# First pair of heads loaded in whole rows and routed in two halves, with a shorter centroid norm and other places for the weight-rounding steps

## The chip, the cores and the metric

One core of a Trainium2 chip runs the whole kernel. The metric is the device time of one execution in microseconds (us), the median of several runs. The engines are named as the profile names them: PE (TensorE, with PEld for its weight loads), DVE (VectorE), ACT (ScalarE), POOL (GpSimd) and SP (the queue from which most DMAs are issued).

## The reference

Routing attention is followed by an MLP mixer. The attention has batch 4, 8 heads, 768 positions and head size 64. Each head has 16 centroids, and a query sees only the keys that have the same nearest centroid.

```python
c_n = centroids / (np.linalg.norm(centroids, axis=-1, keepdims=True) + 1e-06)
q_assign = np.argmax(np.einsum('bhsd,hcd->bhsc', q_n, c_n), axis=-1)
k_assign = np.argmax(np.einsum('bhsd,hcd->bhsc', k_n, c_n), axis=-1)
mask = q_assign[:, :, :, None] == k_assign[:, :, None, :]
scores = np.where(mask, scale * np.matmul(q, k.transpose(0, 1, 3, 2)), -1000000000.0)
attn = softmax(scores)          # written out in the reference
x = np.matmul(attn, v)          # then (B, S, H*D) = (4, 768, 512)
u = x + (np.maximum(x.transpose(0, 2, 1) @ w_tok1, 0.0) @ w_tok2).transpose(0, 2, 1)
out = u + np.maximum(u @ w_ch1, 0.0) @ w_ch2
```

Here q_n and k_n are q and k divided by their norms (which does not change the argmax), w_tok1 is 768x256, w_tok2 256x768, w_ch1 512x1536 and w_ch2 1536x512.

## The kernel before

The order of all instructions is written out by hand. Each engine works its own queue in that order.

**Pairs and groups.** Attention works on 16 pairs (a batch and two heads, both on the 128 partitions of a tile). A pair is done in four groups, numbered m over the whole kernel: g = m // 4 is the pair and s = m % 4 the step in it. Groups s = 0 and 1 handle the first half of the queries (qh = 0) with key chunks 0 to 2 and 3 to 5; s = 2 and 3 do the same for the second half. One group m issues, on PE, the score matmuls of three key chunks (scores, L377: a bf16 product of one-hot tiles "ohT" that sets the mask, then the fp32 product of q and k from "qkT"); on ACT, their exponentials (L383); on DVE, the sum of the exponentials of group m - 1 (add_up, L394 and L398); and on PE the product of those exponentials with v (values, L408). Scores live in a PSUM pool of three two-bank buffers, tag "sc", which are taken in turn; a fourth tile in some groups ("small" at s = 1, "px" at s = 2) shifts the turn by one, so that the third score block of the next group takes the buffer that this tile had.

**Routing of the next pair** runs beside the groups of the present one. At s = 0 turn transposes q and k in 32x32 blocks on DVE (L287). At s = 1 route_products multiplies them with the centroids (L299, into small). At s = 2 route takes the products through a DVE transpose (L316), a maximum (L320) and comparisons (L324) to one-hot rows, and counts the keys' entries on ACT (L331); then route_turn transposes the one-hots by a DMA on SP. The output of the previous pair is finished at the same steps: denominators into small (L425) at s = 1, their transpose (dent, L429) and reciprocal at s = 2, the transposes of the output (px, L438) at s = 2, and half_out (L446), which reads px on DVE, at the start of s = 3. load(g + 2) issues the loads of the pair after next at s = 1.

**Weights** are rounded beside attention. A step of weight_steps issues one raw load on SP for one piece, two ACT instructions (L200, L202) for the piece before it, and three DVE instructions (L207, L212, L217) and one POOL addition (L224) for the one before that. There are 19 pieces in the first list, hence 21 steps. A step is issued at the end of a group:

```python
if m < last - GROUPS:
    n = m % WEVERY == 0 or m == 1
else:
    n = m % 2 if m < last else 2
```

with WEVERY = 3, last = 64 and GROUPS = 4.

**The start.** begin loads the centroids and the first pair, computes the centroids' norm with an integer first guess and three Newton rounds (centroids_norm, L241 to L278), and routes the first pair ahead of group 0: turn for k, products, turn for q, route for k, products for q, and so on, with PE transposes of the one-hots (route_turn_first, L347) in place of the DMA. The first pair's loads are like all others: head size is split in two, so that a quarter of the partitions takes rows of 32 numbers (128 bytes). Matmuls on zeros (keep_warm, L729) stand between the steps.

After attention come the token products (tok1, L478; tok2, L487) and the channel products (L609, L660).

Of the kernel before, what the change touches and what calls it, by code (L numbers as in the profile page):

```python
# [17 lines left out]
C = 16  # L18
P = 128
# [15 lines left out]
GROUPS = 2 * NJ // NG  # L35
WEVERY = 3
SM_SCALE = 0.125
# [10 lines left out]
def kernel(  # L48
# [70 lines left out]
    rcps = const.tile([P, NPAIR, 2, 2, HJ], F32, name="rcps")  # L119
    cells = const.tile([P, NPAIR], F32, name="cells")  # L120

# [9 lines left out]

    def load(g, queues=None):


        b, f = divmod(g, NF)
        st = state.setdefault(g, {})
        st["qk"] = qkpool.tile([P, 2, NJ, NQ, QP], F32, name="qk")
        st["va"] = loads.tile([P, 2, NJ, D], F32, name="va")
        for a, src in ((1, k), (0, q)):
            queue = queues[a] if queues else nc.sync  # L140
            for c in range(NQ):
                h, d0 = 2 * f + c // 2, (c % 2) * QP
                queue.dma_start(
                    st["qk"][c * QP : (c + 1) * QP, a].rearrange("r j i d -> r (j i) d"),
                    src[b, h, :, d0 : d0 + QP].rearrange("(i r j) d -> r j i d", i=NQ, j=NJ),
                )
# [94 lines left out]
    def centroids_norm(cen):  # L241
        sq = rsmall.tile([P, D], F32, name="censq")
        ss = rsmall.tile([P, 1], F32, name="ss")
        nc.vector.tensor_tensor(out=sq, in0=cen, in1=cen, op=ALU.mult)
        nc.vector.reduce_sum(out=ss, in_=sq, axis=AX.X)

        lo = rsmall.tile([P, 1], F32, name="lo")
        nc.vector.tensor_scalar_max(out=lo, in0=ss, scalar1=float(2.0**-100))
        nrm = rsmall.tile([P, 1], F32, name="nrm0")
        nc.vector.tensor_scalar(  # L250
            out=nrm.bitcast(I32), in0=lo.bitcast(I32), scalar1=0.5, scalar2=float(0x1FBD1DF5),
            op0=ALU.mult, op1=ALU.add,
        )
        for it in range(3):
            rr = rsmall.tile([P, 1], F32, name="rr")
            nc.vector.reciprocal(out=rr, in_=nrm)
            tw = rsmall.tile([P, 1], F32, name="tw")
            nc.vector.scalar_tensor_tensor(
                out=tw, in0=ss, scalar=rr, in1=nrm, op0=ALU.mult, op1=ALU.add
            )  # L260
            nrm = rsmall.tile([P, 1], F32, name="nrm")
            nc.vector.tensor_scalar(
                out=nrm, in0=tw, scalar1=0.5, scalar2=(1e-6 if it == 2 else 0.0),
                op0=ALU.mult, op1=ALU.add,
            )
        rden = rsmall.tile([P, 1], F32, name="rden")
        nc.vector.reciprocal(out=rden, in_=nrm)
        cn = rsmall.tile([P, 2, D], F32, name="cn")
        for i in range(2):
            nc.vector.tensor_scalar_mul(out=cn[:, i], in0=cen, scalar1=rden)  # L270
        pc = ps_sc.tile([P, H * C], F32, tag="sc", name="pc")
        nc.tensor.transpose(out=pc, in_=cn.rearrange("p i d -> p (i d)"), identity=ident)
        nc.vector.tensor_copy(out=cnT, in_=pc)
        nc.vector.memset(cnd, 0.0)
        for i in range(2):
            rows = slice(i * D, (i + 1) * D)
            nc.vector.tensor_copy(
                out=cnd[rows, :, i], in_=cnT.rearrange("p (f i c) -> p f i c", f=NF, i=2)[rows, :, i]  # L278
            )


    def turn(g, kinds=(1, 0)):
        st = state[g]
        if 1 in kinds:
            st["T"] = qktp.tile([P, 2, NJ, P], F32, name="qkT")
        for a in kinds:
            nc.vector.transpose(  # L287
                out=st["T"][:, a].rearrange("p j t -> p (j t)"),
                in_=st["qk"][:, a].rearrange("p j i d -> p (j i d)"),
            )  # L290

    def route_products(g, a0=0, a1=2, pr=None):

        st, f = state[g], g % NF
        if pr is None:
            pr = ps_sc.tile([P, (a1 - a0) * NJ * QP], F32, tag="sc", name="pr")
        for i in range(NQ):
            rows = slice(i * QP, (i + 1) * QP)
            nc.tensor.matmul(  # L299
                pr[rows], lhsT=cnd[:, f].rearrange("p i c -> p (i c)"),  # L300
                rhs=st["T"][:, a0:a1, :, rows].rearrange("p a j r -> p (a j) r"),
                start=True, stop=True,
            )
        st["pr"] = pr

    def route(g, a0=0, a1=2):

        st = state[g]
        NR = (a1 - a0) * NJ * 2
        sc = rsmall.tile([P, NR, C], F32, name="sim")
        nc.vector.transpose(  # L316
            out=sc.rearrange("p n c -> p (n c)"), in_=st.pop("pr")
        )
        mx = rsmall.tile([P, NR], F32, name="mx")
        nc.vector.reduce_max(out=mx, in_=sc, axis=AX.X)  # L320
        for a in range(a0, a1):
            oh = ohs[g % 2][:, a].rearrange("p j (h x) -> p j h x", h=2)[:, :, :, 0:C]
            n = slice((a - a0) * 2 * NJ, (a - a0 + 1) * 2 * NJ)
            nc.vector.tensor_tensor(  # L324
                out=oh, in0=sc[:, n].rearrange("p (j h) c -> p j h c", h=2),
                in1=mx[:, n].rearrange("p (j h) -> p j h", h=2).unsqueeze(3)
                .to_broadcast([P, NJ, 2, C]),
                op=ALU.is_lt if a else ALU.is_ge,
            )
            if a:  # L330
                nc.scalar.activation(  # L331
                    out=rsmall.tile([P, NJ, 2, C], BF16, name="others"), in_=oh, func=ACT.Copy,
                    accum_out=cells[:, g : g + 1],
                )
            else:
                nc.vector.tensor_scalar_mul(out=oh, in0=oh, scalar1=-BIG)

# [8 lines left out]

    def route_turn_first(a):  # L347

        st, oh = state[0], ohs[0]
        if a == 1:  # L350
            st["ohT"] = qktp.tile([P, 2, NJ, P], BF16, name="ohT")
        po = ps_sc.tile([P, NJ, P], BF16, tag="sc", name="po")
        for j in range(NJ):
            nc.tensor.transpose(out=po[:, j], in_=oh[:, a, j], identity=identb)
        if a == 0:
            nc.vector.tensor_copy(out=st["ohT"][:, 0], in_=po)
        else:
            nc.scalar.copy(out=st["ohT"][:, 1], in_=po)

# [6 lines left out]
    def scores(m):  # L366
# [4 lines left out]

        for chunks in (range(NG - 1), (NG - 1,)):
            for src, start in ((st["ohT"], True), (st["T"], False)):
                for i in chunks:
# [307 lines left out]
    def fits():  # L682
# [4 lines left out]
        for i, (src, limit, op) in enumerate(  # L687
            (
                (flat, LIMIT, ALU.is_le),
                (flat, 1.0 / LIMIT, ALU.is_ge),  # L690
                (cells, float(2 * NJ * (C - 1)), ALU.is_equal),
            )
# [18 lines left out]
    def begin():  # L711
        cen = rsmall.tile([P, D], F32, name="cen")
        nc.sync.dma_start(cen, centroids.rearrange("h c d -> (h c) d"))
        load(0, (nc.scalar, nc.sync))

        nc.vector.memset(ones, 1.0)
        warm = rsmall.tile([P, WMAX], BF16, name="warm")
        nc.vector.memset(warm, 0.0)
        nc.scalar.activation(out=rsmall.tile([P, QP], F32, name="expd"), in_=ones, func=ACT.Exp)
        make_identity(nc, ident)  # L720
# [6 lines left out]
        def keep_warm(n):  # L727
            for _ in range(n):
                nc.tensor.matmul(pw, lhsT=warm[:, 0:P], rhs=warm[:, P : P + HS], start=True, stop=True)  # L729

        keep_warm(12)
        centroids_norm(cen)
        keep_warm(7)
        turn(0, (1,))
        route_products(0, 1, 2)
        turn(0, (0,))
        route(0, 1, 2)
        keep_warm(1)
        route_products(0, 0, 1)
        keep_warm(2)  # L740
        route_turn_first(1)
        route(0, 0, 1)
        keep_warm(1)
        route_turn_first(0)

# [9 lines left out]
    for m in range(last + 3):  # L755
# [3 lines left out]
        if s == 2:  # L759
            if old >= 0:  # L760
                pair_denominators(old)
            if more:
                route(g + 1)
            if old >= 0:
                pair_reciprocals(old)
        if s == 3 and old >= 0:
            for qh in range(2):
                half_out(old, qh)
        if more and s == 0:
            turn(g + 1)  # L770
        if 1 <= m <= last:
            add_up(m - 1)
        if m < last:
            scores(m)
        if 1 <= m <= last:
            values(m - 1)
        if m < last and s == 1:
# [3 lines left out]
            if more:  # L781
                route_products(g + 1, pr=two[:, 1, 0:HS])
        if more and s == 2:
# [24 lines left out]
        if m < last - GROUPS:  # L808
            n = m % WEVERY == 0 or m == 1
        else:  # L810
            n = m % 2 if m < last else 2
# [247 lines left out]
```

## Time and profile before

| | |
|---|---|
| Median of 3 runs | 896.99 us (895.4, 896.99, 897.04) |
| Profiled execution | span 895.3 us |
| PE busy | 873.7 us, 98% of the span |
| DVE, ACT, POOL busy | 499.4, 286.4 and 44.6 us |
| First score matmul | 15.49 us |
| Last of attention's value products | about 352 us |
| Mean granted PE clock | 0.993 of full speed |

A line of the profile gives, in order, the source line, the engine, the instruction, "output<-input" by tile names, the shapes, the count, the busy time and the mean of one, and then the engine's idle time ahead of it with what ended that. A timeline line gives the start and the length in us and then the same names. PE's busy time counts pipelined matmuls with modelled ends, so a high share says that PE is occupied, not that it runs at its peak. PEclk is the share of full clock that PE was granted.

### The profile page before, as it was taken

What the parts mean: (1) busy time and instruction counts of PE and PEld (TensorE: products, weight loads), DVE (VectorE), ACT (ScalarE), POOL (GpSimd) and SP (SyncE); (2) the same over time, 40 slices, a digit from 0 to 9 for tenths busy, and PEclk for the clock granted to TensorE, in tenths of its full rate; (3) what the DMA queues carried; (4) which work ended last, traced back from release to release, by engine and by line L of the source; (5) the groups of instructions that cost most, each with busy time, mean ns of one, the idle gap of its engine ahead of it and who ended that gap; (6) DMA issues with size and microseconds to landing.
All of it is one profiled execution on the core that took longest, in us unless ns stands there. A gap on an engine that the chain in (4) does not pass through costs nothing.

```text
span 895.3 us, 11001 instructions
## 1 busy us (share of the span) xinstructions
PE 873.7 (98%) x4286; PEld 519.4 (58%) x4286; DVE 499.4 (56%) x849; ACT 286.4 (32%) x501; POOL 44.6 (5%) x40
## 2 busy tenths in 40 slices
PE   7999999999999999999999999999999999999996
PEld 3444444444444444444458677686776867768675
DVE  5677778788788776385473434433344333443342
ACT  2554555555556545231120221202212022130210
POOL 1010000010101001140000000000000000000000
PEclk7999999999999999999999999999999999999999
DMA  9654455555665131130000001000010000100001
GB/s 164 138 107 89 89 120 113 112 123 106 106 120 100 40 89 34 61 118 0 1 0 1 1 24 47 1 1 0 17 54 0 1 1 13 59 1 1 0 25 50
DMA packets 136347, 47.61 MB, mean 53 GB/s; under 512 B 125152, under 2 KB 129248, under 8 KB 136288
## 3 DMA queue, kind: packets, MB, share of 16 engines
q1 hardware_dynamic: 133152, 46.45, 23.7%
q10 hardware_dynamic: 3136, 0.39, 0.4%
q8 instruction: 35, 0.57, 0.3%
q14 instruction: 24, 0.20, 0.1%
HBM read 34.64 MB, written 6.29 MB: 46 GB/s over the span
## 4 chain that ended last, share of the span: by engine, by line
PE 93%; DVE 5%; DMA 1%; ACT 0%; issue 0%; DVEq 0%
PE sc L377 16%; PE pX L660 14%; PE pX L609 14%; PE av L408 14%; PE pZ L660 7%; PE pZ L609 7%; PE ph L478 5%; PE pu L487 5%; PE pY L660 3%; PE pY L609 3%; DVE sum L398 2%; PE small L425 1%; PE pt L550 1%; PE small L299 1%; PE px L438 1%; DMA qk<-in_k_dram 1%
## 5 line engine op out<-in xcount | busy, mean ns | idle before, releaser
L383 ACT ACTIVATE ex<-sc 128x768 f32<-128x768 f32 x192 | 144.2, 809 | 59.8 <-PE sc L377 50.3
L377 PE MATMUL sc<-qkT 64*128 64x384 f32 x768 | 146.1, 486 | 0.0
L408 PE MATMUL av<-ex,va 128*64 128x384 f32 x768 | 137.8, 494 | 0.0
L398 DVE TENSOR_TENSOR sum<-sum,ex 128x768 f32<-128x768 f32 x128 | 124.4, 972 | 10.6 <-DVE sum L398 0.5
L408 PEld LDWEIGHTS av<-ex,va 128*64 128x64 f32 x768 | 49.5, 136 | 80.5 <-issue 66.0
L377 PEld LDWEIGHTS sc<-qkT 64*128 64x128 f32 x768 | 70.6, 189 | 34.6 <-issue 13.8
L609 PE MATMUL pX<-uT,wc 128*128 128x384 f32 x192 | 67.4, 487 | 0.0
L377 PE MATMUL sc<-ohT 64*128 64x384 bf16 x384 | 53.4, 329 | 6.0 <-DVE x L446 5.3
L617 ACT COPY p<-pX 128x384 f32<-128x384 f32 x24 | 11.4, 475 | 148.1 <-PE pX L609 148.1
L609 PEld LDWEIGHTS pX<-uT,wc 128*128 128x128 f32 x192 | 36.2, 190 | 24.7 <-issue 1.0
L224 POOL TENSOR_TENSOR wc<-wT,wup 128x512 int32<-128x512 int32 x24 | 32.5, 1354 | 244.4 <-DVE wT L217 194.7
L377 PEld LDWEIGHTS <-ohT 64*128 64x128 bf16 x384 | 13.8, 94 | 49.0 <-issue 32.2
L487 PE MATMUL pu<-h,wt 128*128 128x512 f32 x96 | 42.0, 592 | 0.0
L478 PE MATMUL ph<-x,wt 128*128 128x512 f32 x96 | 42.0, 593 | 0.0
L429 DVE STREAM_TRANSPOSE dent<-small 128x384 f32<-128x384 f32 x15 | 8.7, 583 | 55.9 <-PE small L299 50.5
L504 DVE TENSOR_TENSOR c<-pZ,u 128x384 f32<-128x384 f32 x24 | 13.4, 558 | 47.2 <-PE pZ L609 47.2
L504 DVE TENSOR_TENSOR x<-pX,x 128x256 f32<-128x256 f32 x24 | 10.2, 424 | 49.3 <-PE pX L660 49.3
L504 DVE TENSOR_TENSOR hA<-pY,p 128x384 f32<-128x384 f32 x24 | 13.4, 557 | 40.4 <-PE pY L609 40.4
L660 PE MATMUL pX<-w2s,hA 128*128 128x256 f32 x144 | 35.1, 380 | 0.5 <-DVE x L504 0.5
L660 PE MATMUL pX<-wc,hA 128*128 128x256 f32 x144 | 35.0, 379 | 0.0
L660 PE MATMUL pZ<-w2s,hS 128*128 128x256 f32 x144 | 35.0, 379 | 0.0
L660 PE MATMUL pY<-wc,hA 128*128 128x256 f32 x144 | 35.0, 379 | 0.0
(123 smaller groups left out, 1201.6 us busy)
## 6 DMA issues: line engine op xcount, KB each, us to landing
raw<-in_moe_w_ch_dram SPq DMA_DIRECT2D x24, 512.0 KB, 4.3
qk<-in_k_dram SPq DMA_DIRECT2D x64, 96.0 KB, 4.5
va<-in_v_dram SPq DMA_DIRECT2D x16, 384.0 KB, 3.2
out_dram<-x SPq DMA_DIRECT2D x24, 256.0 KB, 2.0
qk<-in_q_dram SPq DMA_DIRECT2D x60, 96.0 KB, 3.7
raw<-in_moe_w_tok_dram SPq DMA_DIRECT2D x3, 512.0 KB, 5.2
raw<-in_moe_w_tok_dram SPq DMA_DIRECT2D x4, 384.0 KB, 4.1
qk<-in_q_dram ACTq DMA_DIRECT2D x4, 96.0 KB, 4.4
```

Source lines behind the costliest of these rows:

```text
L224: nc.gpsimd.tensor_tensor(out=dst.bitcast(I32), in0=T, in1=up, op=ALU.add)
L299: nc.tensor.matmul(pr[rows], lhsT=cnd[:, f].rearrange("p i c -> p (i c)"), rhs=st["T"][:, a0:a1, :, rows].rearrange("p a j r -> p (a j) r" ...
L377: nc.tensor.matmul(scs[i][:, h, 0:HS], lhsT=src[rows, 1, j0 + i], rhs=src[rows, 0, js], start=start, stop=not start,)
L383: nc.scalar.activation(out=ex, in_=scs[i][:, :, 0:HS], func=ACT.Exp, scale=SM_SCALE)
L398: nc.vector.tensor_tensor(out=acc, in0=acc, in1=ex, op=ALU.add)
L408: nc.tensor.matmul(st["av"][h * D : (h + 1) * D], lhsT=st["va"][:, h, j], rhs=ex[:, h], start=(j == 0), stop=(j == NJ - 1),)
L478: nc.tensor.matmul(pf, lhsT=W["tok1"][:, j, t * P : (t + 1) * P], rhs=xs[b][:, j], start=(j == 0), stop=(j == NJ - 1),)
L487: nc.tensor.matmul(pu, lhsT=W["tok2"][:, t, j], rhs=h1s[b][:, t], start=(t == 0), stop=(t == NT - 1))
L504: nc.vector.tensor_tensor(out=dst, in0=a, in1=b, op=ALU.add)
L609: nc.tensor.matmul(psum, lhsT=A[a][:, k, c * P : (c + 1) * P], rhs=R[r][:, k], start=start and k == 0, stop=k == 1, skip_group_check=not s ...
L617: nc.scalar.copy(out=kept[name], in_=psum)
L660: nc.tensor.matmul(psum, lhsT=h2[a][:, k, i * P : (i + 1) * P], rhs=Bw[w][:, 3 * part + k], start=start and k == 0, stop=k == 2, skip_grou ...
```

## The change

1. **Loads of the first pair.** load_first reads, for each half n of the positions of a row group (three of six), each of k and q and each head, 128 partitions x 3 rows x 64 numbers. k goes out on SP and q on ACT, eight loads in all, half 0 first.
2. **Turning.** turn_first transposes a half of q and k by six PE transposes into PSUM; ACT and DVE copy them to qkT.
3. **Routing in two halves.** Products, maximum, one-hots and PE transposes of the one-hots are done for half 0 ahead of group 0. Half 1's products and comparisons are issued ahead of group 0 too; its one-hots are transposed in second_first, which stands between the second and the third score block of group 0. The factor -BIG is applied when q's one-hots are copied out of PSUM. The counts of both halves come in second_first.
4. **turn(1)** moves from before the scores of group 0 to behind them.
5. **Centroid norm.** Two Newton rounds with other constants in place of three; one multiplication in place of two for cn; cnd is filled straight from PSUM, and its memset stands at the top of begin. The transposed centroids' PSUM tile comes from pool ps_w.
6. **Routing of later pairs.** The one-hots of k come ahead of those of q, then -BIG, then the count.
7. **Rounding steps** are issued at the end of every s = 1, and of s = 3 in the first six pairs.

The diff, cut to its core:

```diff
-WEVERY = 3
+EARLY = 6
...
-        for it in range(3):
+        for it in range(2):
...
-        for i in range(2):
-            nc.vector.tensor_scalar_mul(out=cn[:, i], in0=cen, scalar1=rden)
-        pc = ps_sc.tile([P, H * C], F32, tag="sc", name="pc")
+        nc.vector.tensor_scalar_mul(
+            out=cn, in0=cen.unsqueeze(1).to_broadcast([P, 2, D]), scalar1=rden
+        )
+        pc = ps_w.tile([P, H * C], F32, tag="w", name="pc")
...
+    def load_first():
...
+        for n in range(2):
+            for a, src, queue in ((1, k, nc.sync), (0, q, nc.scalar)):
+                for h in range(2):
+                    queue.dma_start(
+                        st["rows"][:, n, a, :, h],
+                        src[0, h].rearrange("(p j) d -> p j d", p=P)[:, HJ * n : HJ * n + HJ],
+                    )
...
+    def turn_first(n):
...
+        pt = ps_sc.tile([P, 2, 512], F32, tag="sc", name="pt")
+        js = slice(HJ * n, HJ * n + HJ)
+        for a in (1, 0):
+            for j in range(HJ):
+                nc.tensor.transpose(
+                    out=pt[:, a, j * P : (j + 1) * P],
+                    in_=st["rows"][:, n, a, j].rearrange("p h d -> p (h d)"), identity=ident,
+                )
...
+    def second_first():
+
+        po = route_turn_first(1)
+        for a in (1, 0):
+            route_first_out(1, po, a)
+        for n in range(2):
+            route_count(0, slice(HJ * n, HJ * n + HJ), NPAIR * n)
...
         for chunks in (range(NG - 1), (NG - 1,)):
+            if m == 0 and len(chunks) == 1:
+                second_first()
...
         keep_warm(12)
-        centroids_norm(cen)
-        keep_warm(7)
-        turn(0, (1,))
-        route_products(0, 1, 2)
-        turn(0, (0,))
-        route(0, 1, 2)
-        keep_warm(1)
-        route_products(0, 0, 1)
+        pc = centroids_norm(cen)
         keep_warm(2)
-        route_turn_first(1)
-        route(0, 0, 1)
-        keep_warm(1)
-        route_turn_first(0)
+        tq, tk = turn_first(0)
+        nc.scalar.copy(out=tq[0], in_=tq[1])
+        nc.vector.tensor_copy(out=tk[0], in_=tk[1])
+        centroids_out(pc)
+        nc.scalar.copy(out=cnT, in_=pc)
+        keep_warm(2)
+        pr = ps_sc.tile([P, 2, 512], F32, tag="sc", name="pr")
+        route_products(0, pr[:, 0, 0 : HS // 2], js[0])
+        for out, src in turn_first(1):
+            nc.scalar.copy(out=out, in_=src)
+        route(0, js[0])
+        keep_warm(2)
+        po = route_turn_first(0)
+        for a in (1, 0):
+            route_first_out(0, po, a)
+        route_products(0, pr[:, 1, 0 : HS // 2], js[1])
+        route(0, js[1])
...
-        if more and s == 0:
+        if more and s == 0 and m > 0:
             turn(g + 1)
...
             scores(m)
+        if m == 0:
+            turn(1)
...
         if m < last - GROUPS:
-            n = m % WEVERY == 0 or m == 1
+
+            n = s == 1 or s == 3 and g < EARLY
```

More of the change, by code (lines that the diff above doesn't have):

```diff
@@ L119 @@
     rcps = const.tile([P, NPAIR, 2, 2, HJ], F32, name="rcps")
-    cells = const.tile([P, NPAIR], F32, name="cells")
+    cells = const.tile([P, NPAIR + 1], F32, name="cells")
     W = {
@@ L129, with load @@
     xs = [xpool.tile([P, NJ, DM], F32, name=f"x{b}") for b in range(B)]
-    def load(g, queues=None):
+    def load(g):
         b, f = divmod(g, NF)
@@ L139, in load @@
         for a, src in ((1, k), (0, q)):
-            queue = queues[a] if queues else nc.sync
             for c in range(NQ):
                 h, d0 = 2 * f + c // 2, (c % 2) * QP
-                queue.dma_start(
+                nc.sync.dma_start(
                     st["qk"][c * QP : (c + 1) * QP, a].rearrange("r j i d -> r (j i) d"),
@@ L250, in centroids_norm @@
         nc.vector.tensor_scalar(
-            out=nrm.bitcast(I32), in0=lo.bitcast(I32), scalar1=0.5, scalar2=float(0x1FBD1DF5),
+            out=nrm.bitcast(I32), in0=lo.bitcast(I32), scalar1=0.5, scalar2=float(0x1FBB6875),
             op0=ALU.mult, op1=ALU.add,
         )
-        for it in range(3):
+        for it in range(2):
             rr = rsmall.tile([P, 1], F32, name="rr")
@@ L262, in centroids_norm @@
             nc.vector.tensor_scalar(
-                out=nrm, in0=tw, scalar1=0.5, scalar2=(1e-6 if it == 2 else 0.0),
+                out=nrm, in0=tw, scalar1=(0.5, 0.49984956)[1 - it], scalar2=(0.0, 1e-6)[it],
                 op0=ALU.mult, op1=ALU.add,
@@ L268, in centroids_norm, with centroids_out @@
         cn = rsmall.tile([P, 2, D], F32, name="cn")
-        for i in range(2):
-            nc.vector.tensor_scalar_mul(out=cn[:, i], in0=cen, scalar1=rden)
-        pc = ps_sc.tile([P, H * C], F32, tag="sc", name="pc")
+        nc.vector.tensor_scalar_mul(
+            out=cn, in0=cen.unsqueeze(1).to_broadcast([P, 2, D]), scalar1=rden
+        )
+        pc = ps_w.tile([P, H * C], F32, tag="w", name="pc")
         nc.tensor.transpose(out=pc, in_=cn.rearrange("p i d -> p (i d)"), identity=ident)
-        nc.vector.tensor_copy(out=cnT, in_=pc)
-        nc.vector.memset(cnd, 0.0)
+        return pc
+    def centroids_out(pc):
         for i in range(2):
@@ L277, in centroids_norm, with turn @@
             nc.vector.tensor_copy(
-                out=cnd[rows, :, i], in_=cnT.rearrange("p (f i c) -> p f i c", f=NF, i=2)[rows, :, i]
+                out=cnd[rows, :, i], in_=pc.rearrange("p (f i c) -> p f i c", f=NF, i=2)[rows, :, i]
             )
-    def turn(g, kinds=(1, 0)):
+    def turn(g):
         st = state[g]
-        if 1 in kinds:
-            st["T"] = qktp.tile([P, 2, NJ, P], F32, name="qkT")
-        for a in kinds:
+        st["T"] = qktp.tile([P, 2, NJ, P], F32, name="qkT")
+        for a in (1, 0):
             nc.vector.transpose(
@@ L290, in turn, with route_products @@
             )
-    def route_products(g, a0=0, a1=2, pr=None):
+    def route_products(g, pr, js=slice(0, NJ)):
         st, f = state[g], g % NF
-        if pr is None:
-            pr = ps_sc.tile([P, (a1 - a0) * NJ * QP], F32, tag="sc", name="pr")
         for i in range(NQ):
@@ L300, in route_products @@
                 pr[rows], lhsT=cnd[:, f].rearrange("p i c -> p (i c)"),
-                rhs=st["T"][:, a0:a1, :, rows].rearrange("p a j r -> p (a j) r"),
+                rhs=st["T"][:, :, js, rows],
                 start=True, stop=True,
@@ L304, in route_products, with onehots, route, route_count @@
         st["pr"] = pr
[L306 to L319, printed above, removed]
+    def onehots(g, a, js):
+        return ohs[g % 2][:, a, js].rearrange("p j (h x) -> p j h x", h=2)[:, :, :, 0:C]
+    def route(g, js=slice(0, NJ)):
+        nj = js.stop - js.start
+        sc = rsmall.tile([P, 2 * nj * 2, C], F32, name="sim")
+        nc.vector.transpose(out=sc.rearrange("p n c -> p (n c)"), in_=state[g].pop("pr"))
+        mx = rsmall.tile([P, 2 * nj * 2], F32, name="mx")
         nc.vector.reduce_max(out=mx, in_=sc, axis=AX.X)
-        for a in range(a0, a1):
-            oh = ohs[g % 2][:, a].rearrange("p j (h x) -> p j h x", h=2)[:, :, :, 0:C]
-            n = slice((a - a0) * 2 * NJ, (a - a0 + 1) * 2 * NJ)
+        for a in (1, 0):
+            n = slice(a * 2 * nj, (a + 1) * 2 * nj)
             nc.vector.tensor_tensor(
-                out=oh, in0=sc[:, n].rearrange("p (j h) c -> p j h c", h=2),
+                out=onehots(g, a, js), in0=sc[:, n].rearrange("p (j h) c -> p j h c", h=2),
                 in1=mx[:, n].rearrange("p (j h) -> p j h", h=2).unsqueeze(3)
-                .to_broadcast([P, NJ, 2, C]),
+                .to_broadcast([P, nj, 2, C]),
                 op=ALU.is_lt if a else ALU.is_ge,
             )
[L330 to L336, printed above, removed]
+    def route_count(g, js=slice(0, NJ), column=None):
+        column = g if column is None else column
+        nc.scalar.activation(
+            out=rsmall.tile([P, NJ, 2, C], BF16, name="others")[:, js], in_=onehots(g, 1, js),
+            func=ACT.Copy, accum_out=cells[:, column : column + 1],
+        )
+    def route_big(g):
+        oh = onehots(g, 0, slice(0, NJ))
+        nc.vector.tensor_scalar_mul(out=oh, in0=oh, scalar1=-BIG)
     def route_turn(g):
@@ L345, in route_turn @@
         )
[L347 to L354, printed above, removed]
+    def load_first():
+        st = state[0] = {"qk": qkpool.tile([P, 2, NJ, NQ, QP], F32, name="qk")}
+        st["va"] = loads.tile([P, 2, NJ, D], F32, name="va")
+        st["T"] = qktp.tile([P, 2, NJ, P], F32, name="qkT")
+        st["ohT"] = qktp.tile([P, 2, NJ, P], BF16, name="ohT")
+        st["rows"] = st.pop("qk").rearrange("p a j i d -> p (a j i d)").rearrange(
+            "p (n a j h d) -> p n a j h d", n=2, a=2, h=2, j=HJ
+        )
[5 more added lines that the diff above has]
+                        src[0, h].rearrange("(p j) d -> p j d", p=P)[:, HJ * n : HJ * n + HJ],
+                    )
+        nc.sync.dma_start(st["va"], v[0, 0:2].rearrange("h (p j) d -> p h j d", p=P))
@@ new lines, in turn_first @@
+    def turn_first(n):
+        st = state[0]
+        pt = ps_sc.tile([P, 2, 512], F32, tag="sc", name="pt")
[5 more added lines that the diff above has]
+                    in_=st["rows"][:, n, a, j].rearrange("p h d -> p (h d)"), identity=ident,
+                )
+        return [
+            (st["T"][:, a, js].rearrange("p j t -> p (j t)"), pt[:, a, 0:HS]) for a in range(2)
+        ]
@@ L355, in route_turn_first, with route_first_out @@
+    def route_turn_first(n):
+        po = ps_w.tile([P, 2, HJ, P], BF16, tag="w", name="po")
+        for a in (1, 0):
+            for j in range(HJ):
+                nc.tensor.transpose(
+                    out=po[:, a, j], in_=ohs[0][:, a, HJ * n + j], identity=identb
+                )
+        return po
+    def route_first_out(n, po, a):
+        out = state[0]["ohT"][:, a, HJ * n : HJ * n + HJ]
         if a == 0:
-            nc.vector.tensor_copy(out=st["ohT"][:, 0], in_=po)
-        else:
-            nc.scalar.copy(out=st["ohT"][:, 1], in_=po)
+            nc.vector.tensor_scalar_mul(out=out, in0=po[:, 0], scalar1=-BIG)
+        elif n == 0:
+            nc.scalar.copy(out=out, in_=po[:, 1])
+        else:
+            nc.vector.tensor_copy(out=out, in_=po[:, 1])
@@ L361, in split @@
+    def second_first():
+        po = route_turn_first(1)
+        for a in (1, 0):
+            route_first_out(1, po, a)
+        for n in range(2):
+            route_count(0, slice(HJ * n, HJ * n + HJ), NPAIR * n)
+        nc.vector.tensor_tensor(
+            out=cells[:, 0:1], in0=cells[:, 0:1], in1=cells[:, NPAIR : NPAIR + 1], op=ALU.add
+        )
+        state[0].pop("rows")
     def split(m):
@@ L690, in fits @@
                 (flat, 1.0 / LIMIT, ALU.is_ge),
-                (cells, float(2 * NJ * (C - 1)), ALU.is_equal),
+                (cells[:, 0:NPAIR], float(2 * NJ * (C - 1)), ALU.is_equal),
             )
@@ L713, in begin @@
         nc.sync.dma_start(cen, centroids.rearrange("h c d -> (h c) d"))
-        load(0, (nc.scalar, nc.sync))
+        load_first()
         nc.vector.memset(ones, 1.0)
@@ L718, in begin @@
         nc.vector.memset(warm, 0.0)
+        nc.vector.memset(cnd, 0.0)
         nc.scalar.activation(out=rsmall.tile([P, QP], F32, name="expd"), in_=ones, func=ACT.Exp)
@@ L729, in keep_warm @@
                 nc.tensor.matmul(pw, lhsT=warm[:, 0:P], rhs=warm[:, P : P + HS], start=True, stop=True)
+        js = [slice(0, HJ), slice(HJ, NJ)]
         keep_warm(12)
-        centroids_norm(cen)
-        keep_warm(7)
-        turn(0, (1,))
-        route_products(0, 1, 2)
-        turn(0, (0,))
-        route(0, 1, 2)
-        keep_warm(1)
-        route_products(0, 0, 1)
-        keep_warm(2)
-        route_turn_first(1)
-        route(0, 0, 1)
-        keep_warm(1)
-        route_turn_first(0)
+        pc = centroids_norm(cen)
+        keep_warm(2)
+        tq, tk = turn_first(0)
[11 more added lines that the diff above has]
+        po = route_turn_first(0)
+        for a in (1, 0):
+            route_first_out(0, po, a)
+        route_products(0, pr[:, 1, 0 : HS // 2], js[1])
+        route(0, js[1])
     begin()
@@ L763 @@
                 route(g + 1)
+                route_big(g + 1)
+                route_count(g + 1)
             if old >= 0:
@@ L781 @@
             if more:
-                route_products(g + 1, pr=two[:, 1, 0:HS])
+                route_products(g + 1, two[:, 1, 0:HS])
         if more and s == 2:
```

## The prediction

> **What bounds the kernel now.** First the page's busy times: TensorE leads, at 98% of the span.
>
> ```profile
> PE 873.7 (98%) x4286; PEld 519.4 (58%) x4286; DVE 499.4 (56%) x849; ACT 286.4 (32%) x501; POOL 44.6 (5%) x40
> ```
>
> So a change can only gain where TensorE is idle, slow or doing spare work. The waits of TensorE between 16 and 352 us (the attention stage) hold one entry (us, times, longest):
>
> ```profile
> PE sc L377 <- DVE x L446: 5.3, 5, 1.1
> ```
>
> The timeline shows one of these five stalls, in m = 7 (group 1, step 3):
>
> ```profile
> 50.65 0.42 DVE L207 TENSOR_SCALAR wh<-wh 128x512 f32<-128x512 f32 x1
> 51.11 0.43 DVE L212 TENSOR_SCALAR wh<-wh 128x512 uint32<-128x512 uint32 x1
> 51.62 0.69 DVE L217 SCALAR_TENSOR_TENSOR wT<-raw,wh 128x512 uint32<-128x512 uint32 x1
> 52.23 1.01 DVE L446 TENSOR_TENSOR x<-px,rcps 128x384 f32<-128x384 f32 x2
> 53.30 0.34 PE L377 MATMUL sc<-ohT 64*128 64x384 bf16 x2 [1.11 <-DVE x L446]
> ```
>
> The three rounding instructions of the step issued at the end of m = 6 stand ahead of half_out (L446), which frees the PSUM buffer px that the third score block of m = 7 takes next. Steps fall on m % 3 == 0, so those at m = 6, 18, 30, 42, 54 (the second half of a pair's work, s = 2) are exactly the five. In a pair whose s = 2 has no step:
>
> ```profile
> 69.69 3.02 DVE L398 TENSOR_TENSOR sum<-sum,ex 128x768 f32<-128x768 f32 x3
> 72.63 1.02 DVE L446 TENSOR_TENSOR x<-px,rcps 128x384 f32<-128x384 f32 x2
> ```
>
> half_out is done at 73.65; the timeline has TensorE at its third block at 74.00, without idle. The slack is 0.35 us.
>
> Third, the start. The chain of waits from 0 to 16 us (start, us, what):
>
> ```profile
> 0.74 2.94 DMA qk<-in_q_dram
> 3.68 0.02 issue
> 3.69 5.53 DMA qk<-in_k_dram
> 9.22 0.03 issue
> 9.25 0.99 DVE qkT L287
> ...
> 14.88 0.57 DVE ohT L356
> 15.45 0.04 issue
> 15.49 0.80 PE sc L377 x3
> ```
>
> The first score matmul runs at 15.49 us. 8.5 us of that is transfer in 128-byte rows. Then the clock (windows of 3.41 us; busy, then PEclk):
>
> ```profile
> 5.52:8.93 3.41, 1.44 (x8) 0.74 (x8) 1.39 (x7) 0.00 (x0) 0.00 (x0) 1.00 1.39 175
> 8.93:12.34 3.41, 2.06 (x18) 0.54 (x19) 2.82 (x5) 0.00 (x0) 0.00 (x0) 0.50 1.29 156
> 12.34:15.75 3.41, 2.76 (x21) 1.72 (x19) 2.28 (x7) 1.25 (x3) 0.00 (x0) 0.50 1.05 170
> 15.75:19.17 3.42, 3.42 (x16) 2.11 (x14) 1.48 (x2) 1.07 (x2) 0.00 (x0) 0.50 1.14 275
> ```
>
> A window that was 42% busy is followed by half clock, and only a wholly busy one ends it. So the whole first routing and most of the first scores run at half speed.
>
> **The Trainium skill.** "TensorE: Matmul & The Clock Gate", Part 1, says that the clock is halved by default and after an idle window of about 3.4 us, and full after a busy one, the window running free of the kernel: agreed, with 3.41 us steps above. The same part (Architectural detail) calls VectorE's queue strictly first in, first out; the trace agrees, since half_out sat behind rounding work it doesn't need. "DMA: Bandwidth & Descriptors", in the section on why a DMA increments its semaphore by 16, says that one descriptor moves one contiguous run of the last dimension. The new loads read 768 bytes in a row but write three runs of 256, so I count on 256-byte packets. In this trace a 256-byte packet (centroids, ohT) takes 18 ns at the median against 13 for 128 bytes.
>
> **Part 1, rounding steps.** Both versions issue 21 steps, each one SP DMA, two ScalarE instructions (0.69 + 0.68), three VectorE (0.42 + 0.43 + 0.69 = 1.54) and one GpSimd. They go to the end of every s = 1 (15) and of s = 3 in the first six pairs. s = 2 has none, so the five stalls go: 1.11 + 0.85 + 1.13 + 1.12 + 1.13 = 5.3 us, all on TensorE. New places: at s = 1 VectorE waits for the "small" matmuls anyway; with a step there (m = 9) it still idles 3.24 us before dent at 67.09, and those at m = 21, 33, 45 and 57 leave 3.25 to 3.79. At s = 3 the step stands behind half_out and ahead of turn and add_up; m = 15, 27, 39, 51 have just that, with no TensorE idle. After an s = 3 step the next dent still finds VectorE idle for 4.0 us; a pair with both should leave about 4.0 - 1.6 = 2.4. On SP the raw load stays behind load(g+2) and ahead of route_turn, as at m = 9; on ScalarE the count at s = 2 waits about 4 us for VectorE today, which swallows 1.37. Routing's new order (q's one-hot, then -BIG, the count after) has the same instructions; I cost it at 0, bounds -0.1 to +0.1 per pair, inside the slack of 0.35. Gain 5.3, bounds 4.3 to 5.4.
>
> **Part 2, the start, if the clock stays full.**
> - Loads: eight DMAs of 384 packets (3072 in all, before 6144) on two queues at some 0.65 us an issue. First half issued by 2.5 us; 1536 packets x 18 ns / 16 = 1.7 us; landing near 4.5 (bounds 4 to 6), the second half near 6.
> - Centroid norm: one iteration less (0.16 + 0.22 + 0.15 with gaps = 0.64 us: 4.24 to 4.88), one cn instruction for two (-0.15), cnd's memset into VectorE's idle 1.5 us ahead of cen: cn at 5.36 instead of 6.14.
> - pc 5.45; two warm matmuls (0.16 each) to 5.95; six transposes (px: 6 in 0.82) to 6.8. The copies: VectorE k 0.55 (half_out's shape), ScalarE q 0.49 (avT's shape), two cnd copies 0.39: done at 7.55.
> - Products of half 0 to 8.1; second six transposes to 8.9. VectorE: 0.38 + 0.35 + two one-hots of half width (0.2 to 0.36 each, I take 0.25) with gaps: 9.55.
> - Six bf16 transposes to 10.15, the two ohT copies (half of 0.80 and of 0.56 upward: 0.3 to 0.5) to 10.7, during which the products of half 1 run. **First scores at 10.8, against 15.49: 4.7 earlier.**
> - m = 0: two blocks take about 1.65 at full clock (+0.15 for a PSUM buffer that half 1's transpose frees) to 12.6; second_first's six transposes, on one-hots ready at 12.05, to 13.0; third block 13.8. ScalarE's two counts (0.9) end at 13.0, before the first exponent at 13.1. m = 1 is held 0.8 us by the exponents that free its buffers: scores to 17.0, values to 19.1. turn(1), now behind m = 0 on VectorE, is done by 16 to 17.5, depending on load(1), ahead of its reader at 19.1. In the trace that point is 24.31: 5.2 earlier.
>
> Bounds of what the trace doesn't show: the half-width one-hots, 0.2 to 0.36 each, twice on the path; the PSUM copies of k and q, 0.4 to 0.6; the bf16 copies, 0.28 to 0.56. Together -0.4 to +0.7. No lower end goes below nothing: each is new work on the path, and what pays for it (the two turns, 1.84 us, and the wait for 128-byte rows) is in the 15.49. New waits: TensorE's first transposes wait for the first half's loads, and all of routing stands behind them (the late-transfer rival); second_first waits for half 1's one-hots with only the third block behind it, which needs half 0 alone (0 at full clock: ready 12.05, wanted 12.6); half 1's transposes wait for its loads (0: near 6, wanted 8.1). On SP nine loads stay ahead of load(1), which starts no later than now; on ScalarE four q issues (2.6) and the table load (1.28) end by 4.8, before its first copy near 7. Eighteen warm matmuls instead of 23 and cnT's copy on ScalarE lie beside those waits.
>
> Semaphore delays are priced at 0.05 to 0.1 each on some twelve hand-overs; I take off 0.7 for the slower ones: **4.5**.
>
> If the clock halves again at 8.93, the rest doubles on TensorE: first scores at 12.1, m = 0 ends at 17.3 and the 24.31 point comes at 21.9: gain 2.4 (1.7 to 2.6).
>
> **Sum.** 895.3 - 5.3 - 4.5 = 885.5 in the profiled span. The timed runs (895.4, 896.99, 897.04) lie up to 1.7 above that span; from the median, 896.99 - 9.8 = **887.2 us**. From there to the end nothing is touched.
>
> **The rivals.**
> - Clock falls back (27%). For: the phase is free, and 81% busy was not enough to restore it. Against: I count about 80% busy in both critical windows, where 42% lost it. 896.99 - 5.3 - 2.4 = 889.3.
> - Transfers late (5%): each us past 5.95 is paid in full; landing at 8, as now, gives about 889.2.
> - New stalls in the dense pairs (5%): VectorE runs without idle from dent to the next group; if the six early s = 3 steps each cost a stall of 0.85 to 1.1, 5 to 6.6 us return: about 892.5. Against: the four precedents.
> - The other side (3%): half_out becomes late everywhere. Place: s = 2 and 3 of 15 pairs, slack 0.35. A delay d costs 15 x (d - 0.35), so it eats the whole 9.8 from d = 1.0; a full step in the way (1.54) costs 17.9, giving 905. That needs a step at s = 1 to reach past dent, 3.2 us later; the trace speaks against it.
> - The stalls or the start don't change (2%), because TensorE is held by something else: about 896.
>
> Likeliest (58%): 887.2, own range 885.6 to 888.8. The range that takes in the half clock is 885.4 to 890.4. 0.2% is 1.8 us, about what a measurement of this kernel can tell from no change. Faster 0.94, same 0.03, slower 0.03.
>
> **What would show it.** Right: no TensorE wait on x L446 in the attention stage; first scores near 11; the m = 1 products near 19; PEclk 1.00 past 8.93. Half steps: first scores near 12 at PEclk 0.50. Wrong: TensorE idle at s = 0 or s = 3 with VectorE as releaser; transposes waiting for qk's DMA; dent late after a step.

## The result and the profile after

The changed kernel takes 886.28 us (median of 5 runs, 886.09 to 887.05) against 896.69 us before (median of 5, 895.40 to 897.04): ratio 0.9888, 95% interval 0.9873 to 0.9902. That is 10.4 us less, where 9.8 was forecast. The profiled spans differ by 895.3 - 884.2 = 11.1 us; the profiled execution of the kernel before was one of its longer ones (897.32 us timed).

The page's busy times of the changed kernel:

```profile
PE 869.9 (98%) x4293; PEld 519.0 (59%) x4293; DVE 492.1 (56%) x847; ACT 289.3 (33%) x507; POOL 42.2 (5%) x40
```

The share of TensorE says nothing, as before. The waits of TensorE from 0 to 345 us do (us, times, longest):

```profile
PE pr L298 <- DVE cnd L279: 1.3, 1, 1.3
PE av L783 <- DVE warm L771: 1.2, 1, 1.2
PE sc L430 <- DVE ohT L393: 0.4, 1, 0.4
PE pc L273 <- DVE cn L269: 0.4, 1, 0.4
```

The five waits on half_out (now L499) are gone, and all that is left lies before the first scores. The chain of waits shows what sets the start now (start, us, what; norm left out):

```profile
0.74 2.08 DMA cen<-in_centroids_dram
...
5.95 0.33 PE av L783 x2
6.27 0.67 PE pt L373 x6
6.94 0.02 issue
6.96 0.49 ACT qkT L790
7.45 0.02 issue
7.47 0.56 DVE qkT L791
...
10.88 0.49 ACT ohT L395
...
11.39 0.37 DVE ohT L393
```

The loads of q and k are no longer on it: it runs from the centroids through their norm, and then twice through a copy on VectorE that starts only when ScalarE's copy has ended (qkT, then ohT). The timeline has the marks:

```profile
11.80 0.50 PE L430 MATMUL sc<-ohT 64*128 64x384 bf16 x4 [0.43 <-DVE ohT L393]
...
19.38 0.85 PE L298 MATMUL small<-qkT,cnd 128*32 128x384 f32 x8
...
341.08 15.72 PE L531 MATMUL ph<-x,wt 128*128 128x512 f32 x36
```

The same two marks in the kernel before:

```profile
24.31 0.85 PE L299 MATMUL small<-qkT,cnd 128*32 128x384 f32 x8
...
352.26 15.72 PE L478 MATMUL ph<-x,wt 128*128 128x512 f32 x36
```

First scores at 11.80 instead of 15.49; the "small" products of m = 1 at 19.38 instead of 24.31. The windows of 3.41 us (busy, then PEclk, DMA share, GB/s) show no half clock:

```profile
5.52:8.93 3.41, 1.99 (x19) 1.33 (x19) 0.91 (x3) 0.74 (x2) 0.00 (x0) 1.00 1.09 206
8.93:12.34 3.41, 2.85 (x32) 1.87 (x30) 2.08 (x7) 1.61 (x5) 0.00 (x0) 1.00 0.95 129
```

In the dense pairs VectorE has the slack that was worked out. This is the pair with a step at s = 3 ahead of it and one at its s = 1:

```profile
60.88 0.58 DVE L482 STREAM_TRANSPOSE dent<-small 128x384 f32<-128x384 f32 x1 [2.41 <-PE small L298]
...
63.48 3.02 DVE L451 TENSOR_TENSOR sum<-sum,ex 128x768 f32<-128x768 f32 x3
66.41 1.02 DVE L499 TENSOR_TENSOR x<-px,rcps 128x384 f32<-128x384 f32 x2
```

2.41 us of idle time ahead of dent (2.4 predicted), and dent to half_out takes 5.53 us, against 5.54 (67.09 to 72.63) in the pair shown before: routing's new order costs nothing.

**Where the time went.** The small products come 24.31 - 19.38 = 4.93 us earlier. The first token product (ph), just behind attention, comes at 341.08 instead of 352.26, 11.18 earlier. So 4.93 us are from the start, 6.25 from the rest of attention, and nothing is added later (543.1 us to the end of the span, 543.0 before).

### The profile page after: what moved, and what is told of

The parts are those of the page before. It is cut to its first block, busy times and chain, and to the rows that moved or that the text cites. A ratio compares the mean times of both kernels' runs of the same rounds, so it can differ in the third digit from the quotient of the medians.

```text
span 884.2 us, 11022 instructions
## 1 busy us (share of the span) xinstructions
PE 869.9 (98%) x4293; PEld 519.0 (59%) x4293; DVE 492.1 (56%) x847; ACT 289.3 (33%) x507; POOL 42.2 (5%) x40
## 2 busy tenths in 40 slices
DMA packets 133275, 47.61 MB, mean 54 GB/s; under 512 B 122080, under 2 KB 126176, under 8 KB 133216
## 4 chain that ended last, share of the span: by engine, by line
PE 97%; DVE 1%; ACT 1%; DMA 0%; issue 0%; DVEq 0%
PE sc L430 18%; PE av L461 15%; PE pX L713 14%; PE pX L662 14%; PE pZ L713 7%; PE pZ L662 7%; PE ph L531 5%; PE pu L540 5%; PE pY L713 4%; PE pY L662 4%; PE px L491 1%; PE small L478 1%; PE pt L603 1%; PE small L298 1%; ACT uT L606 0%; DMA cen<-in_centroids_dram 0%
## 5 line engine op out<-in xcount | busy, mean ns | idle before, releaser
L451 DVE TENSOR_TENSOR sum<-sum,ex 128x768 f32<-128x768 f32 x128 | 121.1, 946 | 10.6 <-DVE sum L447 0.5
L223 POOL TENSOR_TENSOR wc<-wT,wup 128x512 int32<-128x512 int32 x24 | 30.7, 1278 | 262.1 <-DVE wT L216 262.1
L557 DVE TENSOR_TENSOR c<-pZ,u 128x384 f32<-128x384 f32 x24 | 13.4, 557 | 46.9 <-PE pZ L662 46.9
L557 DVE TENSOR_TENSOR x<-pX,x 128x256 f32<-128x256 f32 x24 | 10.2, 423 | 49.3 <-PE pX L713 49.3
L557 DVE TENSOR_TENSOR hA<-pY,p 128x384 f32<-128x384 f32 x24 | 13.4, 557 | 40.1 <-PE pY L662 40.1
```

The source lines that it names most:

```text
L223: nc.gpsimd.tensor_tensor(out=dst.bitcast(I32), in0=T, in1=up, op=ALU.add)
L451: nc.vector.tensor_tensor(out=acc, in0=acc, in1=ex, op=ALU.add)
L557: nc.vector.tensor_tensor(out=dst, in0=a, in1=b, op=ALU.add)
```

## The experiments

Two theories stood against each other. **Place and start:** the steps gain because none stands ahead of half_out, whatever their number; the start gains by earlier scores and by full clock, independently. **Density and transfers:** the steps' spacing matters, or they need the new start; the start's gain is the loads' alone.

### 1. Changed kernel, old places of the steps

```diff
-            n = s == 1 or s == 3 and g < EARLY
+            n = m % 3 == 0 or m == 1
```

> The changed kernel with the rounding steps back on every third group (and m = 1). Place theory: the five px stalls come back, each about 1.1 us of TensorE idle and some 0.2 us more for refilling, 6.2 us in all: about 892.5 us, and the start (m = 2's scores near 20.2 us) stays. Rival, that the steps gain nothing by themselves and all of the gain is the start's: about 886.5.

Measured: 892.33 us, 6.05 more than the changed kernel. The waits of TensorE from 5 to 345 us have the old entry again:

```profile
PE sc L430 <- DVE x L499: 5.3, 5, 1.1
```

### 2. Kernel before, new places of the steps

```diff
-            n = m % WEVERY == 0 or m == 1
+            n = s == 1 or s == 3 and g < 6
```

> The kernel before with only the new places of the rounding steps. Place theory: no wait of TensorE on half_out, 6.2 us less than before: about 890.5 us, first scores still at 15.5. Rival, that the steps need the changed start to fit (VectorE late after a dense first pair): little gain, 895 to 897, with stalls elsewhere.

Measured: 889.76 us, ratio to the kernel before 0.9930 (0.9915 to 0.9946), with no wait on half_out. The steps don't need the new start. The medians differ by 7.0, more than 6.2, for a reason that experiment 4 bears on: the runs of the kernel before fall in two groups about 2 us apart (of the 27 beside experiments 1 to 4, nine at 894.8 to 895.4 and eighteen at 896.7 to 897.8; of the 17 beside the later ones, eleven in the lower), and so do these (889.07 to 889.11 and 890.40 to 891.48). Group against group the gain is about 6. A measure that leaves the start out is the stretch from the small products of m = 1 to the first token product: 327.95 us in the kernel before and 327.89 in experiment 1, 321.76 here and 321.70 in the changed kernel. The new places are worth 6.2 us with either start.

### 3. As many steps, as dense, at s = 2 and s = 0

```diff
-            n = s == 1 or s == 3 and g < EARLY
+            n = s == 2 or s == 0 and g < EARLY
```

> The changed kernel with the steps at the end of every s = 2, and of s = 0 in the first six pairs: as many steps, as dense. Place theory: a stall in each of the 14 later pairs that have a step at s = 2 and an output to finish, 1.2 to 1.3 us each: 16.5 to 18 us more, about 903. Rival, that density or spacing matters and not the place: within 1 us of the changed kernel, about 886.5.

Measured: 903.74 us, 17.46 more than the changed kernel. The same view:

```profile
PE sc L430 <- DVE x L499: 15.2, 14, 1.1
```

Fourteen stalls instead of none, with the same 21 steps: place decides, not density. Each costs 17.46 / 14 = 1.25 us, of which the view shows 15.2 / 14 = 1.09.

### 4. Kernel before, TensorE kept busy in its start

```diff
-        keep_warm(7)
+        keep_warm(22)
...
-        keep_warm(1)
+        keep_warm(3)
...
-        keep_warm(2)
+        keep_warm(5)
...
-        keep_warm(1)
+        keep_warm(3)
         route_turn_first(0)
+        keep_warm(3)
```

> The kernel before with more matmuls on zeros in the start, so that TensorE is never idle for long (22, 3, 5, 3 and 3 in place of 7, 1, 2, 1 and 0). Clock theory: PEclk stays 1.00 past 8.93 us, the first scores move little (by 0.3 to 0.6 us), and m = 0 and 1 run at full speed, so m = 2's scores come 1.8 to 2.4 us earlier than 25.1: about 894.5 us. Rival, that the start's gain is all transfer and order: below 0.5 us, about 896.5.

Measured: 895.06 us (21 runs), ratio 0.9990 (0.9983 to 0.9997). The windows of its profile are at full clock throughout (the second of them: 3.41 of 3.41 us busy, PEclk 1.00), and its timeline has

```profile
21.68 0.85 PE L299 MATMUL small<-qkT,cnd 128*32 128x384 f32 x8
```

2.63 us ahead of the 24.31 in the profile of the kernel before. Some 0.45 of this is not the clock: k landed earlier in this profile, so that VectorE's first transpose began at 8.80 instead of 9.25. The clock's part is thus about 2.2 of the 4.93 us against that profile, and 21.68 - 19.38 = 2.3, with up to 0.45 more, is left for loads, order and norm.

But the median moved by 1.7 only, and eight of the 21 runs stayed at 896.4 to 896.8; group against group the gain is 0.3 and 0.7. Experiment 2's profile (889.11 us, the lower group) shows how that can be. There the old start came to full clock at 13.4 us and kept it, where the profile before (the upper group) had full clock early and then half from 8.9 to 19.2. Its products took 0.87 us against 0.53 here, its second one-hot transposes 0.51; PEclk can't be read there, since the trace has no record of the clock ahead of the first full window. Its small products came at 22.23, 2.08 ahead of the profile before, about as far as the groups are apart, and only 0.55 behind this experiment. So the clock's part depends on the run of the kernel before that one compares with.

That the clock's phase makes the groups in every run is inferred from these two profiles and not shown. Of the eighteen upper runs fourteen were granted 0.991 to 0.995 of full clock on average, of the lower nine none less than 0.995; but the other four upper runs had 0.997, and the eight late runs of this experiment 0.998, like most of the early ones. That average leaves out the time ahead of the first full window (experiment 2's profile has 0.998), so a late first window is not excluded. No late run of this experiment was profiled, and what held these runs stays open.

### 5. Changed kernel without the three pairs of warm matmuls

```diff
-        keep_warm(2)
         tq, tk = turn_first(0)
...
-        keep_warm(2)
         pr = ps_sc.tile([P, 2, 512], F32, tag="sc", name="pr")
...
-        keep_warm(2)
         po = route_turn_first(0)
```

> The changed kernel without the three pairs of warm matmuls in the new start (the first twelve stay). Clock theory: TensorE is busy less than half of the window from 5.5 to 8.9 us, the clock halves there, first scores come near 12.5 and m = 2's scores near 22.5 instead of 20.2: 2 to 2.5 us more, about 888.6. Rival, that the clock holds without them: within 0.3 us, about 886.3.

Measured: 886.26 us, no change: the forecast of 2 to 2.5 us more missed. The windows show where:

```profile
5.21:8.62 3.41, 1.43 (x15) 0.94 (x15) 1.13 (x4) 0.74 (x2) 0.00 (x0) 0.97 1.18 211
8.62:12.03 3.41, 3.10 (x24) 2.01 (x21) 1.52 (x5) 1.51 (x5) 0.00 (x0) 0.53 1.01 135
12.03:15.45 3.42, 3.41 (x32) 2.13 (x32) 2.30 (x8) 1.98 (x5) 0.00 (x0) 1.00 1.02 207
```

The clock did halve after a window that was 42% busy, as forecast. It came back after one window, in which the work itself filled 3.10 of 3.41 us. From the first products to the first scores it took 3.90 us (8.15 to 12.05) instead of 3.26 (8.54 to 11.80), so the half clock cost about 0.64 us; 0.39 of that came back because the first products no longer stood behind the warm matmuls. Small came at 19.63, 0.25 later. So the filler does keep the clock up here, but what it is worth is small, since the half clock lasted for one window only.

### 6. Changed kernel with three Newton rounds

```diff
-        for it in range(2):
+        for it in range(3):
```

with the old first guess and factors.

> The changed kernel with the old norm of three Newton rounds and its old constants. The chain of waits of the changed start begins at the centroids and runs through the norm, so if the norm binds, one round (0.64 us) is paid in full: first scores at 12.4 instead of 11.8, about 886.9. Rival, that the loads of q and k bind the start: no change, 11.8 and 886.3.

Measured: 886.83 us, 0.55 more; first scores at 12.39, small at 19.97, 0.59 later. The norm binds the start.

### 7 and 8. Separate PSUM tiles for the two copies

Experiment 7 gives k's and q's first transposes a tile each; experiment 8 does so for the one-hots too.

```diff
-        pt = ps_sc.tile([P, 2, 512], F32, tag="sc", name="pt")
+        if n == 0:
+            pts = [ps_sc.tile([P, 2, 512], F32, tag="sc", name=f"pt{a}")[:, 0] for a in range(2)]
+        else:
+            pt = ps_sc.tile([P, 2, 512], F32, tag="sc", name="pt")
+            pts = [pt[:, a] for a in range(2)]
...
-        po = ps_w.tile([P, 2, HJ, P], BF16, tag="w", name="po")
+        pk = ps_w.tile([P, HJ, P], BF16, tag="w", name="po")
+        po = ps_av.tile([P, HJ, P], BF16, tag="av", name="po")
+        po = [po, pk]
```

> The changed kernel with k's and q's first transposes in two PSUM tiles in place of one. In the changed trace VectorE's copy of k starts at 7.47, when ScalarE's copy of q out of the same tile ends, though k was ready near 6.6. Shared-tile theory: the copies run side by side, k's copy starts by 6.8, products 0.5 to 0.7 us earlier (8.0 instead of 8.54), first scores at about 11.2: about 885.7. Rival, that k's copy waits for the transposes themselves or for something else: no change, 11.8.

> As the run before it, and the one-hots' transposes also in two tiles, so that the -BIG copy on VectorE does not wait for ScalarE's copy. Shared-tile theory: 0.4 to 0.5 us more, first scores at about 10.8 (what the prediction had): about 885.3. Rival: no change against the run before it.

Measured: 885.23 and 884.78 us, both below every run of the changed kernel. The 0.45 between the two lies within the spread of their runs (884.91 to 885.43 and 884.57 to 885.49). The timeline of experiment 7:

```profile
6.70 0.56 DVE L795 COPY qkT<-pt 128x384 f32<-128x384 f32 x1 [1.28 <-PE pt L377]
...
7.03 0.48 ACT L794 COPY qkT<-pt 128x384 f32<-128x384 f32 x1 [2.65 <-PE pt L377]
...
7.77 0.53 PE L298 MATMUL pr<-qkT,cnd 128*32 128x192 f32 x8 [0.45 <-DVE cnd L279]
```

VectorE's copy no longer waits for ScalarE's; the products come at 7.77 instead of 8.54. In experiment 8 the wait of TensorE on ohT is gone too; its profiled execution kept half clock until 7.1 us, so its 11.13 for the first scores is not to be compared with the 11.03 of experiment 7.

### 9. Split tiles, cnd ahead of k's copy

```diff
-        nc.vector.tensor_copy(out=tk[0], in_=tk[1])
         centroids_out(pc)
+        nc.vector.tensor_copy(out=tk[0], in_=tk[1])
```

> Split PSUM tiles for both kinds of transposes, and the two copies to cnd ahead of VectorE's copy of k, into the time in which VectorE waits for the transposes. If the products wait for VectorE's chain (k's copy 0.56, then cnd 0.45), they now wait for the later of k's copy on VectorE and q's on ScalarE: 0.2 to 0.3 us earlier than with the split alone, about 884.5. Rival, that the products wait for q's copy or the warm matmuls: no change, 884.8.

Measured: 884.67 us, ratio to the kernel before 0.9874 (0.9853 to 0.9894), the lowest median here; products at 7.33, first scores at 10.09, small at 17.67. Against experiment 8 the 0.1 us of the medians decides nothing. Against the changed kernel it is 1.6 us less.

### 10. All eight loads on SP

```diff
-            for a, src, queue in ((1, k, nc.sync), (0, q, nc.scalar)):
+            for a, src, queue in ((1, k, nc.sync), (0, q, nc.sync)):
```

> The changed kernel with all eight loads of the first pair on SP instead of two queues. If the transfers have slack in the changed start (its chain begins at the centroids, not at q or k), first scores stay at 11.8 and the time at 886.3. Rival, that the two queues are what brings the first half in time: q's first half is issued some 1 us later, and the first transposes wait for it, 0.5 to 1 us more, about 887.

Measured: 886.02 us, first scores at 11.82. The transfers have slack; the second queue is not what makes the start short.

### 11. First transposes ahead of the norm

```diff
-        keep_warm(12)
-        pc = centroids_norm(cen)
-        keep_warm(2)
+        keep_warm(9)
         tq, tk = turn_first(0)
         nc.scalar.copy(out=tq[0], in_=tq[1])
+        pc = centroids_norm(cen)
```

> Split tiles, and the first half's transposes ahead of the centroid norm in TensorE's queue, with nine warm matmuls ahead of them instead of twelve; the copy of k stays behind the norm on VectorE. If the first half has landed by 4.5 to 5 us, the transposes and q's copy lie beside the norm, and only the centroids' transpose and cnd stay ahead of the products: products near 6.9 instead of 7.8, first scores near 10, about 884. Rival, that the loads land later than 5.5 us or that the transposes at half clock hold the centroids' transpose up: no gain or a loss against 884.8.

Measured: 885.29 us (883.68 to 885.59), no gain on the 884.78 of experiment 8. Its timeline:

```profile
5.03 1.51 PE L377 MATMUL pt<-ident,qk 128*128 128x128 f32 x6 [0.73 <-DMA qk<-in_k_dram]
...
6.33 0.42 PE L273 MATMUL pc<-ident,cn 128*128 128x128 f32 x1
```

Here the loads do bind: the first half is there at 5.0 us. The transposes ran at half clock (1.51 us for six against 0.82) and held the centroids' transpose, wanted near 5.4, until 6.33. Full clock came only at 8.9, behind the wait. The nine warm matmuls ended at 4.3, where twelve last until 5.3; whether twelve would have brought full clock in time was not tested.

## Why the prediction was right, and where its sizes were off

- **Rounding steps.** The mechanism was right: five stalls by five steps at s = 2. The term was mis-sized: 5.3 us were summed, 6.25 went in the trace, 6.05 in experiment 1, 1.25 a stall in experiment 3. The idle time in the view counts from the modelled end of the matmul before. With no stall, the next block starts ahead of that end: in the pair without a step the second block's products start at 72.72 and are given 1.45 us, to 74.17, and the third block starts at 74.00. That is 0.17 us a stall that the wait doesn't show; 5.3 + 5 x 0.17 = 6.2. The upper bound of 5.4 was too low for that reason. The two lines of that pair:

```profile
72.72 1.45 PE L377 MATMUL sc<-qkT 64*128 64x384 f32 x8
74.00 0.33 PE L377 MATMUL sc<-ohT 64*128 64x384 bf16 x2
```

- **No new stall.** Right: none in the trace, 2.41 us of slack where 2.4 was worked out, and the reordered route at 0.
- **Loads.** The landing near 4.5 was about half a microsecond early (5.0 in experiment 11), within its bounds; they are off the path, as priced. 256-byte packets are borne out: the page has 3072 fewer under 512 bytes (122080 against 125152), and ScalarE's queue moves the same 0.39 MB in 1600 packets instead of 3136. The late-transfer rival, which didn't come, was misread: it puts today's landing at 8, but the chain of waits shown has k landed at 3.69 + 5.53 = 9.22, and by its own rule that gives 890.5, not 889.2.
- **First scores.** Forecast at 10.8, measured at 11.80. The step that failed is "The copies", VectorE's of k and ScalarE's of q taken side by side, and the two ohT copies likewise: both pairs ran one after the other, each pair out of one PSUM tile, and the first products came at 8.54 where 7.55 was forecast. With a tile for each (experiment 7) they came at 7.77; with experiment 8 the time falls by 1.5 us in all.
- **From there to small.** Forecast 8.3 us, measured 7.58. The hold-up of 0.8 us for m = 1's buffers didn't come: half 0's count ran at 11.25, before half 1's one-hots were there, and the first exponential ran at 13.09, as forecast (13.1), although the scores came 1.0 later. The two misses and the 0.7 us taken off for hand-overs nearly cancel: 4.5 against 4.93. That this sum fits is in part luck.
- **The clock.** The likeliest case came, at full clock. But the rival that it falls back was overpriced: a loss of 2.1 us (a gain of 2.4 in place of 4.5) was forecast, 0.64 measured in experiment 5. The step behind it is "only a wholly busy one ends it", with half clock to the end of the start: a window busy for 3.10 of 3.41 us ended it.

The sum was 9.8 us; 10.4 by the medians and 11.1 by the spans. Both bases, 896.99 us and the profile before, lie in the upper of the kernel's two groups of runs. Against the lower group (median 895.13) the change gains 8.85 us, and against experiment 2's old start it brings the small products forward by 22.23 - 19.38 = 2.85 us only. So the fit rests in part on which runs made the base.

## What to carry to other kernels

Look for what stands ahead of an instruction that frees a buffer in its engine's queue, and move work that can wait to where that engine idles; the same 1.54 us of work was free where VectorE idled for 4.0 us, and cost 1.25 us where the slack was 0.35. In a start-up, follow the chain again after each edit: here it went from loads to the norm and to two copies that shared a PSUM tile, and a further edit (experiment 11) put it back on the loads. Price a stall of a pipelined engine from start to start, not by the idle time that a view shows.

## What was not expected of the hardware

- Two copies out of one PSUM tile, by VectorE and ScalarE from different halves of it, ran strictly one after the other (k's copy from 7.47, when q's ended, with its transposes done some 0.8 us before); in two tiles they overlapped (6.70 and 7.03). The runs show the order and that separate tiles end it, not whether the chip itself would need it.
- The half clock lasted three windows (10.2 us) in the profile of the kernel before and one (3.4 us) in experiment 5, after equally empty windows (1.44 and 1.43 us busy). A window busy for 2.76 us at half clock (81%) did not restore it; one of 2.82 us (83%, in experiment 3's profile, where full clock came at 4.05) and one of 3.10 us (91%, experiment 5) did. At full clock, a window busy for 1.61 us (47%, experiment 6, from 5.33 to 8.74) did not lose it. Busy time here is with the modelled ends of matmuls.
